# Weight conversion through a PSUM bank, ELU in one VectorE pass, weight sums on GpSimd, and conversions dealt out in three places of a step

## The chip, the cores and the metric

The kernel runs on one core of a Trainium2 chip. The metric is the device time of one execution in microseconds (us). Engines are named as the profile names them: PE is TensorE (matmuls; PEld are its weight loads), DVE is VectorE, ACT is ScalarE, POOL is GpSimd, SP is SyncE, which here only issues DMAs. Each engine works through its own instructions in a fixed order; semaphores make it wait for others.

## What is computed

Attention on 4 x 8 heads (576 positions, 64 wide, with rotary angles), and then two layers on the 2304 resulting rows of 512. Both layers have 2048 hidden units and no bias; all is float32, the inputs of the weights float64:

```python
h = x @ w_in                                            # layer 1
g = np.where(h > 0.0, h, np.exp(np.minimum(h, 0.0)) - 1.0)
x = (g @ w_out).astype(np.float32)
h = x @ w_in2                                           # layer 2
g = h - np.tanh(h)
return (g @ w_out2).astype(np.float32)
```

## The kernel before

The program has three parts, one after the other: attention, layer 1 and layer 2. The matmuls take float32 values as a sum of a high and a low part (a cast, and the difference that the cast leaves), so each product is three matmuls. A split is therefore always a pair: a cast on ACT, and a subtraction on POOL (or DVE).

**Layer 1** works in 96 steps, numbered 0 to 95: four groups of 512 hidden units, in each six blocks of 384 tokens, in each four steps of 128 hidden units. In step i, `emit_f1(i)` makes h for that step in a PSUM bank from pool `ps_h` (twelve matmuls, L447), and `emit_f2(i - 4)` multiplies the finished g of four steps earlier by the second weight into four PSUM banks from pool `ps_y` (twelve matmuls, L481). Every fourth step a token block is complete: `emit_acc` in the next step empties the four y banks into `xa`, on ACT in the first group (L491) and by an addition on DVE later (L493), and the next `emit_f2` needs these banks. Between the two, the ELU of step i runs as exp on ACT into one of two buffers `ft` (`emit_act`, L455), two DVE instructions (`emit_dve`, L460 and L461, emitted a step later), and a split (`split_g`, L464 on ACT and L465 on POOL, two steps later) into one of three buffers `gt`.

**Conversion.** All weights come as float64. A chunk of 512 columns is loaded raw (`load_w`, L64, a DMA on SP into one of two buffers in `fm`), and `conv_part` turns it into float32: part 0 takes the magnitude of the high word on ACT (L74), part 1 clamps and shifts (L76, L77), part 2 puts the sign bits in (L81), part 3 adds the low word's bits (L85), the last three parts on DVE. All read and write `GM`, a region of the SBUF tile `fm`. The result is then split into layer 1's weight memory (`conv_w`, L91 and L92), or split and stored in DRAM for layer 2 (`stage_out`, L91 and L92, then `store`, L509). For layer 2's first weight the sums of quarters of two chunks are stored too (`pair_sums`, L518 to L522, on DVE).

The list `todo` holds this conversion work with a due time in steps; in the loop over the steps everything due by i is emitted at the end of step i, after `emit_dve`, in the order of the due times. What the engines get is that order, and each engine keeps it.

**Layer 2** has 24 steps q: three pairs of token blocks, in each eight pairs of weight chunks. It forms products of sums of blocks (a Strassen-like scheme): seven blocks of six matmuls per q (L701) into four banks, and units of twelve matmuls for the second weight (L669). For each of four results per q, `stage_a` (a square, a mask, a polynomial and tanh on ACT and POOL), `stage_b` (DVE, L726 to L730) and `stage_c` (a split) make h - tanh(h). The mask of small h is an is_lt on POOL (L715). The sums of x blocks and their splits for the next pair of token blocks (`combo_sums`, L571 to L577; `combo_split`, L583 and L584) are in a list `todo2` that is filled in the last two of the eight steps of a pair and emitted by `next_combo`, at most four times a step, and the rest at the end of the last.

## Time and profile before

| | us |
|---|---|
| median of 3 runs (1180.15 to 1181.58) | 1180.58 |
| the profiled execution | 1183.5 |
| its span, first to last instruction | 1181.7 |
| PE busy | 1089.3 (92%) |
| DVE busy | 914.3 (77%) |
| POOL busy | 764.4 (65%) |
| ACT busy | 650.9 (55%) |

The profile is of one execution. Its page gives busy time by engine, the chain of work that ended last, and the costliest groups of instructions. The trace behind it answers further questions: busy times in a chosen stretch, who waited for whom and how long, all instructions of a line with their shortest, median and longest duration, and the instructions in order of time. A line number such as L493 is a line of the kernel before. In the rows, "x4" is a count, and a bracket such as [4.06 <-DVE xa L493] says that the engine sat idle for 4.06 us ahead of that instruction and that the named one ended the wait.

### The profile page before, as it was taken

What the parts mean: (1) busy time and instruction counts of PE and PEld (TensorE: products, weight loads), DVE (VectorE), ACT (ScalarE), POOL (GpSimd) and SP (SyncE); (2) the same over time, 40 slices, a digit from 0 to 9 for tenths busy, and PEclk for the clock granted to TensorE, in tenths of its full rate; (3) what the DMA queues carried; (4) which work ended last, traced back from release to release, by engine and by line L of the source; (5) the groups of instructions that cost most, each with busy time, mean ns of one, the idle gap of its engine ahead of it and who ended that gap; (6) DMA issues with size and microseconds to landing.
All of it is one profiled execution on the core that took longest, in us unless ns stands there. A gap on an engine that the chain in (4) does not pass through costs nothing. (4 is left out here: it accounts for less than half of the span.)

```text
span 1181.7 us, 18751 instructions
## 1 busy us (share of the span) xinstructions
PE 1089.3 (92%) x6512; PEld 970.6 (82%) x6512; DVE 914.3 (77%) x1564; ACT 650.9 (55%) x1418; POOL 764.4 (65%) x662
## 2 busy tenths in 40 slices
PE   2999999999979898989999999979997999799998
PEld 2777777777779897979899999979986998688996
DVE  5888878988477888778889867576787778877784
ACT  2676666776645544333344434366666666657662
POOL 2887887876466745444454545576787777866773
PEclk9999999999998999989999999999998999989999
DMA  7767767675023344243343664253544755536531
GB/s 227 225 180 220 180 179 212 182 223 121 19 90 98 125 142 127 77 138 135 132 133 102 211 212 154 87 189 131 173 158 144 266 176 189 180 99 229 197 118 54
DMA packets 80574, 184.27 MB, mean 156 GB/s; under 512 B 7264, under 2 KB 43104, under 8 KB 80480
## 3 DMA queue, kind: packets, MB, share of 16 engines
q1 hardware_dynamic: 80480, 183.07, 49.4%
q8 instruction: 52, 0.85, 0.3%
q14 instruction: 42, 0.34, 0.1%
HBM read 126.94 MB, written 27.79 MB: 131 GB/s over the span
## 5 line engine op out<-in xcount | busy, mean ns | idle before, releaser
L701 PE MATMUL hb<-blk,wa 128*128 128x384 f32 x1008 | 193.6, 341 | 22.9 <-DVE fm L729 20.0
L701 PEld LDWEIGHTS hb<-blk,wa 128*128 128x128 f32 x1008 | 179.9, 190 | 31.5 <-DVE fm L729 21.9
L252 POOL TENSOR_SCALAR a<-a,r 128x576 f32<-128x576 f32 x144 | 134.5, 945 | 63.9 <-DVE r L249 43.6
L465 POOL TENSOR_TENSOR gt<-ft,gt 128x384 fp32r<-128x384 f32 x96 | 111.6, 1163 | 79.4 <-ACT gt L464 66.9
L669 PE MATMUL y<-wb,blk 128*128 128x512 f32 x603 | 156.6, 397 | 1.0 <-ACT blk L464 0.5
L715 POOL TENSOR_SCALAR fm<-fm 128x384 f32<-128x384 f32 x96 | 124.2, 1294 | 50.1 <-ACT fm L714 41.2
L235 ACT ACTIVATE a<-s,nm 128x576 f32<-128x576 f32 x144 | 106.9, 743 | 88.9 <-DVE nm L221 71.6
L455 ACT ACTIVATE ft<-h 128x384 f32<-128x384 f32 x96 | 47.2, 492 | 178.4 <-POOL gt L465 127.7
L221 DVE TENSOR_REDUCE nm<-s 128x1 f32<-128x576 f32 x144 | 108.2, 753 | 37.5 <-PE s L212 35.9
L669 PEld LDWEIGHTS y<-wb,blk 128*128 128x128 f32 x603 | 114.7, 191 | 24.2 <-POOL blk L465 0.9
L481 PE MATMUL y<-gt,wb 128*128 128x384 f32 x576 | 112.5, 344 | 17.6 <-DVE xa L493 16.0
L481 PE MATMUL y<-gt,wa 128*128 128x384 f32 x576 | 112.9, 345 | 12.5 <-ACT xa L491 6.5
L481 PEld LDWEIGHTS y<-gt,wb 128*128 128x128 f32 x576 | 103.6, 194 | 20.2 <-issue 10.2
L481 PEld LDWEIGHTS y<-gt,wa 128*128 128x128 f32 x576 | 104.4, 195 | 14.8 <-ACT xa L491 7.6
L447 PE MATMUL h<-blk,wa 128*128 128x384 f32 x576 | 109.0, 336 | 4.6 <-ACT blk L54 2.6
L447 PE MATMUL h<-blk,wb 128*128 128x384 f32 x576 | 109.3, 338 | 0.0
L92 POOL TENSOR_TENSOR fm<-fm 128x512 fp32r<-128x512 f32 (+1 forms) x48 | 62.7, 1307 | 69.7 <-ACT fm L91 51.0
L447 PEld LDWEIGHTS h<-blk,wa 128*128 128x128 f32 x576 | 100.9, 189 | 6.3 <-ACT blk L54 2.9
L447 PEld LDWEIGHTS h<-blk,wb 128*128 128x128 f32 x576 | 102.7, 191 | 0.0
L76 DVE TENSOR_SCALAR fm<-fm 128x512 f32<-128x512 f32 x64 | 50.0, 781 | 63.1 <-ACT fm L74 62.7
L465 POOL TENSOR_TENSOR blk<-fm,blk 128x384 fp32r<-128x384 f32 x67 | 73.5, 1097 | 37.0 <-ACT blk L464 35.7
L147 POOL TENSOR_TENSOR t<-t,tabs 128x576 f32<-128x576 f32 x59 | 86.7, 1471 | 8.5 <-DMA t<-in_qk 8.5
(103 smaller groups left out, 2284.2 us busy)
## 6 DMA issues: line engine op xcount, KB each, us to landing
wa<-wi SPq DMA_DIRECT2D x96, 448.0 KB, 5.0
wb<-wo SPq DMA_DIRECT2D x48, 512.0 KB, 6.1
k<-hl SPq DMA_DIRECT2D x64, 288.0 KB, 4.4
t<-in_qk SPq DMA_DIRECT2D x30, 576.0 KB, 6.1
wi<-fm SPq DMA_DIRECT2D x24, 512.0 KB, 4.2
fm<-in_w1i SPq DMA_DIRECT2D x16, 512.0 KB, 3.9
fm<-in_w1o SPq DMA_DIRECT2D x16, 512.0 KB, 4.1
fm<-in_w2i SPq DMA_DIRECT2D x16, 512.0 KB, 3.6
```

The lines of the kernel that those rows point to most:

```text
L76: nc.vector.tensor_scalar(out=f, in0=f, scalar1=LO_CLAMP, scalar2=HI_CLAMP, op0=ALU.max, op1=ALU.min)
L92: nc.gpsimd.tensor_tensor(out=lo, in0=f, in1=hi.bitcast(F32), op=ALU.subtract)
L147: eng.tensor_tensor(out=t[:, i, :], in0=t[:, i, :], in1=tabs[:, i, :], op=ALU.mult)
L221: nc.vector.tensor_reduce(out=nm, in_=s_t[i][:, :, 0:288], axis=AX.XY, op=ALU.max, negate=True)
L235: nc.scalar.activation(out=a.rearrange("p (x c) -> p x c", x=2), in_=s[:, :, 0:288], func=AF.Exp, bias=nm_t.pop(i), scale=1.0, accum_out=den,)
L252: nc.gpsimd.tensor_scalar(out=a, in0=a, scalar1=r[:, x:x + 1], scalar2=1.0, op0=ALU.mult, op1=ALU.mult)
L447: nc.tensor.matmul(out=hp, lhsT=w[:, wp, ws], rhs=x_hl(t, xp, c), start=(m == 0), stop=(m == 3 * KC - 1))
L465: nc.gpsimd.tensor_tensor(out=g[:, 1, :], in0=f, in1=g[:, 0, :].bitcast(F32), op=ALU.subtract)
L481: nc.tensor.matmul(out=y_t[e][:, 0:NB], lhsT=w[:, wp, es], rhs=gt[:, gp, :], start=st, stop=sp)
L669: nc.tensor.matmul(out=y, lhsT=gt[:, gp, es], rhs=w[:, wp, :], start=(k == 0), stop=(k == 11))
L701: nc.tensor.matmul(out=bank, lhsT=w[:, wp, o:o + 128], rhs=x[:, xp, cc, :], start=(start and k == 0), stop=(stop and k == 5), skip_group_c ...
L715: nc.gpsimd.tensor_scalar(out=mask, in0=u, scalar1=U_SMALL, scalar2=None, op0=ALU.is_lt)
```

## The change

- **Conversion.** `conv_ps` replaces `conv_part` outside attention: parts 1 and 2 write a PSUM bank `cvb` instead of `GM`, and part 3 writes `GM` from it. The bank is taken from `ps_h`, which keeps three.
- **ELU.** ACT makes relu(-h) and then exp of its negative, into one of three buffers in `fm` (`ft` is gone); DVE makes max(e - 1, h) in one instruction.
- **Sums of weights.** The four instructions go to POOL, each with its own due time.
- **Stores.** `stage_out` puts only the high part into a staging buffer; the low part overwrites its source in `GM`; a store is two DMAs on SP.
- **Loads.** All but the first two raw loads of layer 1 are issued on ACT's queue.
- **Due times.** They are new, and the list is emptied at three places of a step: after `emit_acc`, after `emit_act`, and at the end.
- **Layer 2.** For two of the four results (C22 and C12) the mask is a relu on ACT. `todo2` is filled in the last five steps of a pair, one item in each of the first four, and seven in the last.

```diff
-    fm = const.tile([128, 5888], F32, name="fm")
+    fm = const.tile([128, 6656], F32, name="fm")
...
-    def load_w(key):
+    def load_w(key, eng=nc.sync):
...
-        nc.sync.dma_start(out=t.bitcast(mybir.dt.int64), in_=w_src[l, kind][c])
+        eng.dma_start(out=t.bitcast(mybir.dt.int64), in_=w_src[l, kind][c])
...
-    ps_h = ctx.enter_context(tc.tile_pool(name="ps_h", bufs=4, space=PSUM))
+    ps_h = ctx.enter_context(tc.tile_pool(name="ps_h", bufs=3, space=PSUM))
+    ps_c = ctx.enter_context(tc.tile_pool(name="ps_c", bufs=1, space=PSUM))
...
     def emit_act(i):
-        f = ft[:, i % 2, :]
-        nc.scalar.activation(out=f, in_=h_t[i], func=AF.Exp)
+        f = fm[:, 5376 + NB * (i % 3):5376 + NB * (i % 3) + NB]
+        nc.scalar.activation(out=f, in_=h_t[i], func=AF.Relu, scale=-1.0)
+        nc.scalar.activation(out=f, in_=f, func=AF.Exp, scale=-1.0)
         f_t[i] = f
 
     def emit_dve(i):
         h, f = h_t.pop(i), f_t[i]
-        nc.vector.tensor_scalar(out=f, in0=f, scalar1=1.0, scalar2=-1.0, op0=ALU.min, op1=ALU.add)
-        nc.vector.scalar_tensor_tensor(out=f, in0=h, scalar=0.0, in1=f, op0=ALU.max, op1=ALU.add)
+        nc.vector.scalar_tensor_tensor(out=f, in0=f, scalar=-1.0, in1=h, op0=ALU.add, op1=ALU.max)
+
+    cvb = ps_c.tile([128, 512], F32, name="cvb")
+
+    def conv_ps(key, part, f):
+        words = raw_t[key].bitcast(U32).rearrange("p (n t) -> p n t", t=2)
+        lo_w, hi_w = words[:, :, 0], words[:, :, 1]
+        cu = cvb.bitcast(U32)
+        if part == 0:
+            nc.scalar.activation(out=f, in_=hi_w.bitcast(F32), func=AF.Abs)
+        elif part == 1:
+            nc.vector.tensor_scalar(out=cvb, in0=f, scalar1=LO_CLAMP, scalar2=HI_CLAMP, op0=ALU.max, op1=ALU.min)
+            nc.vector.tensor_scalar(
+                out=cu, in0=cu, scalar1=3, scalar2=0x3FFFFFFF, op0=ALU.logical_shift_left, op1=ALU.bitwise_and
+            )
+        elif part == 2:
+            nc.vector.scalar_tensor_tensor(
+                out=cu, in0=hi_w, scalar=0xC0000000, in1=cu, op0=ALU.bitwise_and, op1=ALU.bitwise_or
+            )
+        else:
+            nc.vector.scalar_tensor_tensor(
+                out=f.bitcast(U32), in0=lo_w, scalar=29, in1=cu, op0=ALU.logical_shift_right, op1=ALU.bitwise_or
+            )
...
-        split_w(st[:, 0, :].bitcast(F32R), st[:, 1, :].bitcast(F32R), GM[:, cols])
-        staged.append((dst, st))
+        split_w(st.bitcast(F32R), GM[:, cols].bitcast(F32R), GM[:, cols])
+        staged.append((dst, st, GM[:, cols]))
...
-        nc.sync.dma_start(out=dst, in_=st)
+        for k, src in enumerate(parts):
+            nc.sync.dma_start(out=dst[:, k, :], in_=src)
...
-        tt = nc.vector.tensor_tensor
...
+        tt = nc.gpsimd.tensor_tensor
...
+    CP = (0, 0.6, 0.8, 1.0)
...
-            todo += [(t0 + 0.35 * (4 * x + k), conv_part, key, k, GM[:, 512 * x:512 * x + 512]) for k in range(4)]
...
+            todo += [(t0 + 1.4 * x + CP[k], conv_ps, key, k, GM[:, 512 * x:512 * x + 512]) for k in range(4)]
...
+            todo += [(t1 + CP[k], conv_ps, key, k, GM[:, at:at + 512]) for k in range(4)]
...
-            while todo and todo[0][0] <= i:
-                _, f, *arg = todo.pop(0)
-                f(*arg)
+            run(i)
...
-            nc.gpsimd.tensor_scalar(out=mask, in0=u, scalar1=U_SMALL, scalar2=None, op0=ALU.is_lt)
+            if v1:
+                nc.scalar.activation(out=mask, in_=u, func=AF.Relu, scale=-1.0, bias=us)
+            else:
+                nc.gpsimd.tensor_scalar(out=mask, in0=u, scalar1=U_SMALL, scalar2=None, op0=ALU.is_lt)
...
-            if live and pr == NPR - 2 and tp + 1 < NT // 2:
...
+            if live and 3 <= pr and tp + 1 < NT // 2:
```

Before `run(i)`, the loop now also has `run(i - 0.67)` after `emit_acc` and `run(i - 0.33)` after `emit_act`.

The order of the instructions shows what the new due times do. On DVE, around the accumulation of step 40, the kernel before has this (L460 and L461 are the ELU, L76 to L85 a conversion, L493 the accumulation):

```order
L460 TENSOR_SCALAR ft<-ft 128x384
L461 SCALAR_TENSOR_TENSOR ft<-h,ft 128x384
L76 TENSOR_SCALAR fm<-fm 128x512
L77 TENSOR_SCALAR fm<-fm 128x512
L81 SCALAR_TENSOR_TENSOR fm<-fm 128x512
L85 SCALAR_TENSOR_TENSOR fm<-fm 128x512
L493 TENSOR_TENSOR xa<-y,xa 128x384 x4
```

The same place in the changed kernel, whose lines are L462 for the ELU, L473, L474, L478 and L482 for the conversion and L517 for the accumulation:

```order
L462 SCALAR_TENSOR_TENSOR fm<-fm,h 128x384
L478 SCALAR_TENSOR_TENSOR cvb<-fm,cvb 128x512
L482 SCALAR_TENSOR_TENSOR fm<-fm,cvb 128x512
L462 SCALAR_TENSOR_TENSOR fm<-fm,h 128x384
L517 TENSOR_TENSOR xa<-y,xa 128x384 x4
L473 TENSOR_SCALAR cvb<-fm 128x512
L474 TENSOR_SCALAR cvb<-cvb 128x512
```

A whole conversion stood directly ahead of the accumulation; now there is one ELU instruction, behind the end of a conversion, and the next conversion begins after it.

On ACT, in steps 39 and 40, the kernel before has (L464 is the cast of g, L455 the exp, L74 the magnitude, L91 a cast of weights):

```order
L464 CAST gt_4272<-ft 128x384
L455 ACTIVATE ft<-h 128x384
L74 ACTIVATE fm<-fm 128x512
L91 CAST fm<-fm 128x512
L464 CAST gt_4272<-ft 128x384
L455 ACTIVATE ft<-h 128x384
L91 CAST wa<-fm 128x512
```

and the changed kernel, with L456 and L457 for relu and exp, L471 for the magnitude, L488 for the cast of g and L64 for a load:

```order
L64 DMA fm<-in_w1o 128x512
L488 CAST gt_4275<-fm 128x384
L456 ACTIVATE fm<-h 128x384
L457 ACTIVATE fm<-fm 128x384
L91 CAST wa<-fm 128x512
L471 ACTIVATE fm<-fm 128x512
L91 CAST fm<-fm 128x512
L488 CAST gt_4275<-fm 128x384
```

The ELU has two instructions instead of one, the loads have come in from SP's queue, and the casts of weights have moved by one place.

On DVE in layer 2, in the next to last step of a pair of token blocks, the kernel before has these (L571, L573 and L575 are the sums of x; L687 an accumulation; L726 to L730, L817 and L829 work on the results):

```order
L687 TENSOR_TENSOR xa<-y,xa 128x4x128
L571 TENSOR_TENSOR ft<-xa 128x768
L817 TENSOR_TENSOR fm<-hb,fm 128x384
L573 TENSOR_TENSOR xa<-xa 128x2x384
L726 TENSOR_TENSOR fm<-fm 128x384
L729 TENSOR_TENSOR fm<-fm 128x384
L730 COPY_PREDICATED fm<-fm 128x384
L687 TENSOR_TENSOR xa<-y,xa 128x4x128
L575 TENSOR_TENSOR xa<-xa 128x2x384
```

In the changed kernel that step has one sum, L597 (formerly L575), between two results:

```order
L761 COPY_PREDICATED fm<-fm 128x384
L597 TENSOR_TENSOR xa<-xa 128x2x384
L757 TENSOR_TENSOR fm<-hb,fm 128x384
L759 SCALAR_TENSOR_TENSOR fm<-fm 128x384
L760 TENSOR_TENSOR fm<-hb,fm 128x384
L761 COPY_PREDICATED fm<-fm 128x384
L715 TENSOR_TENSOR xa<-y,xa 128x4x128
L849 TENSOR_TENSOR fm<-hb,fm 128x384
```

The other two sums have gone to the two steps ahead of it.

## Rows read from the trace of the kernel before

**Rows 1.** Stretches: busy us (instructions) of PE, PEld, DVE, ACT, POOL; clock, DMA.

```profile
320.80:759.04 438.24, 404.79 (x2246) 398.90 (x2246) 345.20 (x518) 181.24 (x368) 231.04 (x191) 0.97 0.40 131
628.16:661.44 33.28, 33.28 (x193) 33.28 (x193) 30.43 (x48) 13.87 (x27) 18.88 (x15) 1.00 0.46 159
502.40:512.69 10.29, 6.23 (x26) 5.94 (x26) 8.34 (x14) 4.02 (x9) 5.52 (x5) 0.75 0.56 181
```

**Rows 2.** Waits of PE in layer 1: us in total, times, longest.

```profile
PE y L481 <- DVE xa L493: 20.8, 11, 4.1
PE y L481 <- ACT xa L491: 8.1, 4, 2.6
PE h L447 <- ACT blk L54: 2.6, 1, 2.6
PE h L447 <- POOL blk L55: 2.0, 2, 1.4
```

**Rows 3.** In order of time, around step 40: start, duration, engine, line, operation.

```profile
503.07 0.49 ACT L455 ACTIVATE ft<-h 128x384 f32<-128x384 f32 x1 [1.95 <-POOL gt L465]
...
504.14 0.43 DVE L76 TENSOR_SCALAR fm<-fm 128x512 f32<-128x512 f32 x1 [3.23 <-ACT fm L74]
...
505.07 1.63 DVE L81 SCALAR_TENSOR_TENSOR fm<-fm 128x512 uint32<-128x512 uint32 x1
...
508.02 1.94 DVE L493 TENSOR_TENSOR xa<-y,xa 128x384 f32<-128x384 f32 x4
...
508.71 4.18 PE L481 MATMUL y<-gt,wb 128*128 128x384 f32 x12 [4.06 <-DVE xa L493]
```

**Rows 4.** The longest waits of ACT and of DVE in layer 1.

```profile
ACT ft L455 <- POOL gt L465: 127.7, 68, 3.9
...
DVE fm L76 <- ACT fm L74: 62.7, 37, 4.1
```

**Rows 5.** Groups of DVE in layer 1: count, busy us, mean ns, idle before.

```profile
L460 DVE TENSOR_SCALAR ft<-ft 128x384 f32<-128x384 f32 x96 | 56.8, 591 | 16.6 <-ACT ft L455 16.6
...
L81 DVE SCALAR_TENSOR_TENSOR fm<-fm 128x512 uint32<-128x512 uint32 x56 | 49.2, 879 | 1.4
...
L76 DVE TENSOR_SCALAR fm<-fm 128x512 f32<-128x512 f32 x56 | 42.5, 760 | 63.1 <-ACT fm L74 62.7
...
L521 DVE TENSOR_TENSOR fm<-fm 128x256 f32<-128x256 f32 x8 | 7.2, 896 | 0.0
```

**Rows 6.** Single lines in layer 1: shortest/median/longest ns, first and last start.

```profile
L76 DVE TENSOR_SCALAR fm<-fm x56: 416/920/1125, 324.5 to 719.4; 128x512 f32<-128x512 f32 x56
...
L81 DVE SCALAR_TENSOR_TENSOR fm<-fm x56: 681/693/1666, 326.1 to 722.5; 128x512 uint32<-128x512 uint32 x56
...
L465 POOL TENSOR_TENSOR gt<-ft,gt x94: 999/1146/1742, 325.7 to 755.5; 128x384 fp32r<-128x384 f32 x94
...
L92 POOL TENSOR_TENSOR fm<-fm x48: 844/1291/2078, 338.9 to 726.2; 128x512 fp32r<-128x512 f32 x40, 128x256 fp32r<-128x256 f32 x8
```

**Rows 7.** SP's loads of raw weights: waits, and issues (ns, shortest/median/longest).

```profile
L64 SPq EVENT_SEMAPHORE  x80: 17/3804/34552, 295.0 to 707.4; - x80
L64 SPq DMA_DIRECT2D fm<-in_w2o x16: 327/328/339, 406.9 to 709.3; - x16
```

**Rows 8.** Stretches of layer 2, columns as in rows 1.

```profile
759.04:805.62 46.58, 38.84 (x199) 35.82 (x199) 28.58 (x49) 27.72 (x57) 30.39 (x27) 0.96 0.40 141
821.26:852.54 31.28, 31.28 (x157) 28.22 (x157) 23.69 (x39) 20.66 (x43) 23.61 (x21) 1.00 0.54 186
868.18:886.14 17.96, 16.19 (x79) 14.02 (x79) 15.65 (x23) 11.52 (x23) 15.34 (x12) 1.00 0.30 103
886.14:910.68 24.54, 18.09 (x80) 15.93 (x80) 17.85 (x25) 14.07 (x28) 18.99 (x14) 0.86 0.45 153
```

**Rows 9.** In order of time, a change of token pair in layer 2.

```profile
888.71 2.20 DVE L729 TENSOR_TENSOR fm<-fm 128x384 f32<-128x384 f32 x1 [0.91 <-POOL fm L719]
...
898.66 2.29 PE L701 MATMUL hb<-blk,wa 128*128 128x384 f32 x6 [6.45 <-DVE fm L729]
```

More of the change, by code (lines that the diff above doesn't have):

```diff
@@ L428, in attention_elu_tanhshrink @@
     gt3 = fcst.tile([128, 3, 2, NB], F32R, name="gt3")
-    ft = fcst.tile([128, 2, NB], F32, name="ft")
     acc = xa
@@ L515, in pair_sums @@
         s1, s2, s3 = (GM[:, 1024 + 256 * k:1280 + 256 * k] for k in range(3))
[L516 to L522 removed]
+        tt = nc.gpsimd.tensor_tensor
+        out_, a, b, op = (
+            (s1, a21, a22, ALU.add), (s2, s1, a11, ALU.subtract), (s3, a11, a21, ALU.subtract), (a21, a12, s2, ALU.subtract)
+        )[part]
+        tt(out=out_, in0=a, in1=b, op=op)
     def pair_out(pr, part):
@@ L541, in attention_elu_tanhshrink @@
             key = (1, 0, 2 * pr + x)
-            todo += [(t0 + 0.35 * (4 * x + k), conv_part, key, k, GM[:, 512 * x:512 * x + 512]) for k in range(4)]
-        todo += [(t0 + 2.8 + 0.3 * k, pair_sums, k) for k in range(2)]
-        todo += [(t0 + (3.4, 4.6, 5.7, 6.8)[k], pair_out, pr, k) for k in range(4)]
-        for o, at in ((3.5, 0), (5.3, 768), (6.7, 0), (8.0, 1280), (9.3, 768)):
+            todo += [(t0 + 1.4 * x + CP[k], conv_ps, key, k, GM[:, 512 * x:512 * x + 512]) for k in range(4)]
+        todo += [(t0 + 2.75 + 0.4 * k, pair_sums, k) for k in range(4)]
+        todo += [(t0 + (3.96, 4.8, 6.3, 7.65)[k], pair_out, pr, k) for k in range(4)]
+        for o, o2, at in ((4.1, 5.55, 1792), (5.7, 7.0, 0), (7.0, 8.35, 768), (8.2, 9.45, 1280), (9.4, 10.65, 1792)):
             t1 = t0 + o
@@ L550, in attention_elu_tanhshrink @@
                 key = lone_b.pop(0)
-            todo += [(t1 + 0.25 * k, conv_part, key, k, GM[:, at:at + 512]) for k in range(4)]
-            todo.append((t1 + 1.25, conv_w, key, 4, at) if key[0] == 0 else (t1 + 1.25, wo_out, key[2], at))
-    todo += [(x[0] + 0.9, store) for x in todo if x[1] in (pair_out, wo_out)]
+            todo += [(t1 + CP[k], conv_ps, key, k, GM[:, at:at + 512]) for k in range(4)]
+            todo.append((t0 + o2, conv_w, key, 4, at) if key[0] == 0 else (t0 + o2, wo_out, key[2], at))
+    todo += [(x[0] + 0.8, store) for x in todo if x[1] in (pair_out, wo_out)]
     todo.sort(key=lambda x: x[0])
-    order = [x[2] for x in todo if x[1] == conv_part and x[3] == 0]
-    free = [x[0] + 0.2 for x in todo if x[1] == conv_part and x[3] == 3]
-    todo += [(0, load_w, key) for key in order[:2]] + [(t1, load_w, key) for t1, key in zip(free, order[2:])]
+    order = [x[2] for x in todo if x[1] == conv_ps and x[3] == 0]
+    free = [x[0] + 0.3 for x in todo if x[1] == conv_ps and x[3] == 3]
+    todo += [(0, load_w, key, nc.sync) for key in order[:2]] + [(t1, load_w, key, nc.scalar) for t1, key in zip(free, order[2:])]
     todo.sort(key=lambda x: x[0])
@@ L561, in x2 @@
         return xa.rearrange("p (c n) -> p c n", n=NTOK)[:, 2 * k:2 * k + 2, NB * t:NB * t + NB]
-    tms = [fm[:, 0:2 * NB].rearrange("p (a n) -> p a n", a=2), ft, ft]
+    tms = [fm[:, o:o + 2 * NB].rearrange("p (a n) -> p a n", a=2) for o in (0, 5760, 5760)]
     XORD = ("B11", "B21", "T2", "T1", "T3", "T4", "B22")
@@ L619, in attention_elu_tanhshrink @@
         nc.vector.memset(b1, B1)
+        nc.vector.memset(us, U_SMALL)
         nc.vector.memset(g1, G1)
@@ L624, in attention_elu_tanhshrink, with run @@
                (combo_split, 0, "T4", nc.vector), (combo_split, 0, "B22", nc.gpsimd)]
+        def run(until):
+            while todo and todo[0][0] <= until:
+                _, f, *arg = todo.pop(0)
+                f(*arg)
         for i in range(n):
@@ L627, in attention_elu_tanhshrink @@
             emit_acc()
+            run(i - 0.67)
             if i < NJ * (NT - 1):
@@ L632, in attention_elu_tanhshrink @@
             emit_act(i)
+            run(i - 0.33)
             if i >= 1:
                 emit_dve(i - 1)
-            while todo and todo[0][0] <= i:
-                _, f, *arg = todo.pop(0)
-                f(*arg)
+            run(i)
             if i >= n - 11:
@@ L647, in attention_elu_tanhshrink @@
         nq = len(qs)
-        banks = [ps_h.tile([128, 512], F32, tag="h", name="hb")[:, 0:NB] for _ in range(4)]
+        banks = [ps_h.tile([128, 512], F32, tag="h", name="hb")[:, 0:NB] for _ in range(3)] + [cvb[:, 0:NB]]
         tl = {}
```

29 lines of the change are left out of this document (12 added, 17 removed).

## The prediction

> **What bounds the kernel now.** I looked first at TensorE's stretch for layer 1, then at what it waits for there, then at one wait in order of time, and last at layer 2. Layer 1 runs from 320.80 to 759.04 us, 438.24 us [rows 1]. Eight of its steps without a stall take 33.28 us, 4.16 each, with TensorE never idle and the granted clock at 1.00, the 2.4 GHz level [rows 1]. Of the steps in the window, numbers 1 to 3 hold twelve matmuls (half a step, 2.08) and 4 to 95 hold twenty-four, so the same matmuls without a stall would take 3 x 2.08 + 92 x 4.16 = 389.0 us. **49.3 us are lost**, and TensorE is the bound otherwise: a gain can only come from these stalls. The list of its waits names them: 20.8 us for DVE's accumulation L493, 8.1 for ACT's accumulation L491, 2.6 and 2.0 for a block of x [rows 2], together 33.5. The rest is the clock after a stall: step 40 takes 10.29 us instead of 4.16, so 6.13 lost, of which 4.06 is the wait, at a mean granted clock of 0.75, between the 1.2 and the 2.4 GHz level [rows 1, 3]. That is 1.51 us lost per us waited, and 33.5 x 1.51 = 50.6, the 49.3 to within 3%. So all of the loss hangs on these waits.
>
> Why the accumulation is late is seen at step 40 [rows 3]. ACT's exp waits 1.95 us for POOL, which still reads the `ft` buffer that exp wants to write. The magnitude pass L74 stands behind it on ACT, DVE's first conversion instruction L76 sits idle 3.23 us for it, and then four conversion instructions run in one piece (504.14 to 508.02) ahead of L493. TensorE gets the y bank 4.06 us late. The totals have the same shape: ACT's exp waits 127.7 us for POOL over layer 1, DVE's L76 62.7 us for ACT [rows 4].
>
> **What the change takes from each engine in layer 1.** DVE is busy 345.2 us [rows 1]. L460 goes: 56.8 us. The pair sums go to POOL: four groups of eight, the costliest 7.2 us, 21.2 together. The four conversion instructions now take 49.2 (L81), 48.8, 47.0 and 42.5 (L76), together 187.5 [rows 5]. Through PSUM they remain four; no row shows a tensor_scalar into PSUM. Bounds: 0.416, the fastest L76, and 0.92, its median [rows 6]. I take 0.69, since L81 runs the same 512 columns in 0.681 at its fastest, close to its median of 0.693; that makes 56 x 4 x 0.69 = 154.6. DVE comes to 345.2 - 56.8 - 21.2 - 187.5 + 154.6 = 234 us (166 to 286 by the bounds), 60% of 389.
>
> The medians say more than the minima: L76 takes 0.416 at its fastest and 0.92 as a rule, and POOL's split L465 0.999 and 1.146 [rows 6]: both engines hold each other up. The Trainium skill (SBUF — State Buffer, Who interferes with whom) says that a DVE instruction with at most one SBUF input and outside the two-port modes does not contend with GpSimd; the conversions with one PSUM side are of that kind, and what the rows show agrees with the other half of the rule, that in-place SBUF ones do contend. By that rule the 0.69 is firm.
>
> ACT gets a second pass for the ELU, 96 x 0.49 = 47.0 (the exp's duration [rows 3]), and issues 54 loads, 0.328 each by SP's row [rows 7] (bounds 0 and 0.66, twice that), 17.7: 181.2 + 47.0 + 17.7 = 246 us of 389, 63%. POOL gets 32 sums of 256 columns at 0.844, the fastest L92 [rows 6] (0.999 at most, L465's 384 columns): 27 us on 231.0, 66%. No engine is full.
>
> **What lies on the path.** An accumulation costs TensorE nothing if DVE is free for it about 1.5 us into its step: TensorE has 2.08 us of `emit_f1` before the first bank is needed, and one of four accumulations takes about 0.5 (L493 x4 in 1.94 us [rows 3]). After the change at most half a conversion stands ahead of one, as the order around step 40 shows: there a single L462 and a finished conversion. The worst case I find in the order is step 32: h at 2.08, relu 0.49, exp 0.49, magnitude 0.66 (exp's 0.49 scaled from 384 to 512 columns), then two DVE instructions of 0.69: 5.1 us after step 31 began, 0.95 us into step 32, in time. At step 52 a cast stands ahead as well and takes it to about 1.6, 0.1 late. So DVE's 20.8 x 1.51 = 31 us go nearly whole. The waits for ACT and for x, 12.7 x 1.51 = 19 us, lie in the first 28 steps; the third ELU buffer takes away the 127.7 us for which ACT stood before POOL, but ACT also gets the relu and the loads there. I leave a quarter of it, 5 us. **Layer 1: 49.3 - 5 = 44 us gained**, bounds 22 (rival A) and 49.3.
>
> At nothing I cost these. Three h banks instead of four: a bank is asked for again 3 x 4.16 - 2.08 = 10.4 us after its matmuls instead of 14.6, and DVE reads it one step later; the list of waits has no matmul that waits for it [rows 2]; without that cover each us late costs 1.51. Two DMAs for a store, and lo halves that stay in GM until they have landed: SP has lost the loads, and a GM region is asked for over a step later; without the cover ACT waits, as rival A prices. The constant `us` is one memset.
>
> **Layer 2** takes 15.64 us per step when nothing stalls (31.28 for two [rows 8]). At a change of token pair it takes 17.96 and 24.54 us, so 2.3 and 8.9 are lost, twice. The change moves two of the three DVE sums that stand in the step before (L571, L573) one and two steps earlier, and one split on POOL three steps earlier. I take the 2.3 for gone, 4.6 in all, since each of these steps now has one extra instruction instead of three. The 8.9 I leave: its four last splits stay in one step, where DVE's L729 takes 2.20 us and TensorE then waits 6.45 us for an L729 [rows 9]; what stands there on DVE and POOL is not touched. Half of the masks move from POOL to ACT, some 0.5 us twice per step (exp's 0.49 [rows 3]). Two undisturbed steps have ACT busy 20.66 of 31.28 us [rows 8]; with four masks 22.7. I cost this at nothing but the last step, 0.5 us; if the chain ACT to DVE had no slack it would be 24 x 0.5 = 12. The start of layer 2 (46.58 us [rows 8]) I leave as it is. **Layer 2: 4.6 - 0.5 = 4 us**, bounds -8 and +13 (half of the 8.9 twice on top).
>
> **Sum.** 44 + 4 = 48 us. The profiled execution took 1183.5 us, so it would take 1135.5; it is 2.9 over the median of 1180.58, and from the median the forecast is 1132.5.
>
> **Rivals.** *A: ACT's queue takes DVE's place.* The loads now stand on ACT, each waiting for DVE's last conversion instruction, and relu and exp behind it; the magnitude pass waits for the load's landing there too. For it: on SP the same loads waited a median of 3.8 us [rows 7]. Against it: they stand a third of a step after the instruction they wait for. If half of layer 1's 44 us stay, 1180.6 - 22 - 4 = 1154.5.
>
> *B: the conversions gain nothing from PSUM.* The Trainium skill (VectorE: DVE Perf Modes, Why PSUM operands drop a tier) says that fp32 with a PSUM operand falls to the single rate; the fastest L76 at 0.416 against L81's 0.681 [rows 6] agrees that there is a double rate to lose. As a mechanism of this kernel: the two tensor_scalars rise by 0.27 each over what they take now, so DVE is at 345.2 - 56.8 - 21.2 + 56 x 0.54 = 297 us, 76%, and first halves of 2 us instead of 1.4 pass the 1.5 us at some accumulations. A third of DVE's 31 us would stay: 1142.5.
>
> *C: the crossings ease too*, since POOL has fewer masks there and DVE comes to them less late. With half of 8.9 gone twice: 1123.5.
>
> *D: slower than before.* If every load holds ACT as long as it held SP, 54 x 3.8 = 205 us, ACT needs 246 + 205 = 451 us for layer 1, more than the 438.2 of now: 1180.6 + 13 - 4 = 1189.5. It decides from (438.2 - 246) / 54 = 3.6 us per load on. Against it: most of SP's wait is its having reached the load early, which the later place takes away.
>
> *E: nothing happens*, because the stalls at the accumulations have a cause that I do not see: 1180.
>
> **How the numbers follow.** Forecast 0.60 (its own range 1124 to 1145), A 0.17, B 0.08, C 0.06, D 0.05, E 0.04. The range 1120 to 1156 takes in the forecast, B, nearly all of C and the nearer half of A, about 0.8. A measurement of this kernel tells 0.2%, some 2.4 us, from no change: faster 0.91, same 0.04, slower 0.05.
>
> **What would show it.** Right: steps of 4.16 us nearly throughout layer 1 and a stretch of about 394 us; no wait of a y matmul for DVE over 1 us; conversion instructions at 0.69 with median and minimum together; no wait of ACT for POOL ahead of the ELU; two stalls at the crossings instead of four. Wrong: L64 or L471 on ACT waiting microseconds with relu behind them (A, D); tensor_scalars over 0.9 in PSUM (B); h matmuls waiting for DVE (the three banks); layer 2's undisturbed steps over 15.64.

## The result and the profile after

The changed kernel takes **1133.24 us** (median of 4 runs, 1132.62 to 1133.92); the kernel before takes 1181.08 beside it. The ratio is 0.9594, 95% interval 0.9577 to 0.961: 4% faster. The profiled run took 1133.38 us with a span of 1131.6. The forecast was 1132.5, in a range of 1120 to 1156.

These are the stretches of the changed kernel that answer to [rows 1] and [rows 8], with the same columns: layer 1, step 40, the step before the first change of token pair, the step of the change, and an undisturbed step of layer 2.

```profile
321.82:712.54 390.72, 389.77 (x2245) 388.91 (x2245) 237.06 (x390) 230.01 (x464) 233.13 (x222) 1.00 0.46 147
479.18:483.34 4.16, 4.16 (x25) 4.16 (x25) 3.90 (x7) 2.77 (x6) 3.34 (x3) 1.00 0.36 137
821.54:837.40 15.86, 15.86 (x79) 14.05 (x79) 14.51 (x22) 12.02 (x25) 11.97 (x9) 1.00 0.35 116
837.40:861.09 23.69, 17.39 (x80) 15.34 (x80) 17.77 (x23) 15.41 (x30) 14.48 (x11) 0.86 0.45 159
1043.24:1058.88 15.64, 15.64 (x79) 14.11 (x79) 11.38 (x19) 12.11 (x26) 9.54 (x9) 1.00 0.69 251
```

Layer 1 is 390.72 us long, down from 438.24: 1.8 us above the 389.0 of matmuls without a stall, where 49.3 were lost. Step 40 is back from 10.29 us to 4.16. The clock of the stretch is 1.00, the 2.4 GHz level, instead of 0.97. Layer 2, from 712.54 us to the end, takes 419.04 us instead of 422.67. With a start of layer 1 that came 1.0 us later, the gain in span is 47.5 + 3.6 - 1.0 = 50.1 us, from 1181.7 to 1131.6. The medians differ by 47.8 us; the profiled execution of the kernel before was 2.9 us above its median.

The waits of TensorE in layer 1 (us in total, times, longest), all that is left of [rows 2]:

```profile
PE h L448 <- POOL blk L55: 0.6, 1, 0.6
PE h L448 <- ACT blk L54: 0.2, 1, 0.2
```

Both stand in one place, step 4; the eleven waits for VectorE's accumulation and the four for ScalarE's are gone. The other two engines of [rows 4], ScalarE and VectorE in the same stretch:

```profile
ACT fm L456 <- PE h L448: 110.4, 77, 1.8
ACT gt L488 <- PE y L505: 13.0, 24, 0.8
ACT fm L456 <- POOL gt L489: 7.5, 4, 3.4
ACT fm L456 <- POOL fm L543: 7.2, 4, 1.8
...
DVE cvb L473 <- ACT fm L471: 95.9, 48, 4.7
DVE fm L462 <- ACT fm L457: 30.4, 18, 3.6
DVE xa L517 <- PE y L505: 11.4, 7, 3.0
```

ScalarE stood 127.7 us waiting for GpSimd's split of g ahead of the ELU, now 7.5; another 7.2 us are new, behind the sums of weights that GpSimd has got (L543). The prediction had announced that none would be left; no accumulation is late for these. ScalarE now stands 110.4 us for the h matmuls, and VectorE stands 11.4 us for the y matmuls ahead of its accumulation: they wait for TensorE and not it for them. VectorE's waits for the magnitude pass grew from 62.7 to 95.9 us and cost nothing: none of TensorE's waits stands behind them.

In order of time around step 40, which begins at 479.18 us, as in [rows 3]:

```profile
474.32 0.55 DVE L462 SCALAR_TENSOR_TENSOR fm<-fm,h 128x384 f32<-128x384 f32 x1
...
477.82 2.12 DVE L517 TENSOR_TENSOR xa<-y,xa 128x384 f32<-128x384 f32 x4 [2.95 <-PE y L505]
...
479.18 2.24 PE L448 MATMUL h<-blk,wb 128*128 128x384 f32 x12
...
479.86 0.68 DVE L473 TENSOR_SCALAR cvb<-fm 128x512 f32<-128x512 f32 x1
...
480.57 0.70 DVE L474 TENSOR_SCALAR cvb<-cvb 128x512 uint32<-128x512 uint32 x1
...
481.26 2.24 PE L505 MATMUL y<-gt,wb 128*128 128x384 f32 x12
481.31 0.69 DVE L478 SCALAR_TENSOR_TENSOR cvb<-fm,cvb 128x512 uint32<-128x512 uint32 x1
```

No conversion stands ahead of the accumulation any more. VectorE is done with an ELU instruction, sits idle 2.95 us for the first y bank, and begins to accumulate at 477.82, 1.36 us before step 40 begins; in the kernel before it began 5.62 us into the step. The next conversion follows it, and the y matmuls start at 481.26, right behind the h matmuls.

### The profile page after: what moved, and what is told of

Same layout as the page of the kernel before. It is cut to its first block, busy times and chain, and to the rows that moved or that the text cites. A ratio compares the mean times of both kernels' runs of the same rounds, so it can differ in the third digit from the quotient of the medians.

```text
span 1131.6 us, 18884 instructions
## 1 busy us (share of the span) xinstructions
PE 1075.9 (95%) x6512; PEld 962.2 (85%) x6512; DVE 801.9 (71%) x1437; ACT 724.2 (64%) x1562; POOL 704.9 (62%) x646
## 4 chain that ended last, share of the span: by engine, by line
PE 74%; DVE 15%; ACT 5%; issue 2%; DMA 1%; POOL 1%; SPq 1%; DVEq 0%; ACTq 0%; POOLq 0%
PE y L505 18%; PE h L448 17%; PE y L697 11%; PE o L326 8%; PE hb L729 7%; PE s L212 6%; PE pt L292 4%; PE cvb L729 3%; DVE nm L221 2%; DVE fm L760 2%; DVE fm L757 2%; DVE fm L761 2%; DVE fm L759 1%; DVE xa L715 1%; DMA k<-hl 1%
## 5 line engine op out<-in xcount | busy, mean ns | idle before, releaser
L489 POOL TENSOR_TENSOR gt<-fm,gt 128x384 fp32r<-128x384 f32 x119 | 124.1, 1043 | 60.9 <-ACT gt L488 58.1
L729 PE MATMUL hb<-blk,wa 128*128 128x384 f32 x720 | 142.3, 342 | 7.3 <-DVE fm L760 6.9
L729 PEld LDWEIGHTS hb<-blk,wa 128*128 128x128 f32 x720 | 129.3, 191 | 12.9 <-DVE fm L760 8.6
L456 ACT ACTIVATE fm<-h 128x384 f32<-128x384 f32 x96 | 47.3, 493 | 126.1 <-PE h L448 110.4
L505 PE MATMUL y<-gt,wb 128*128 128x384 f32 x576 | 107.6, 334 | 1.3 <-DVE xa L517 1.3
L473 DVE TENSOR_SCALAR cvb<-fm 128x512 f32<-128x512 f32 x56 | 38.9, 695 | 98.4 <-ACT fm L471 95.9
L505 PE MATMUL y<-gt,wa 128*128 128x384 f32 x576 | 107.7, 334 | 0.1
L750 POOL TENSOR_TENSOR fm<-fm 128x384 f32<-128x384 f32 x48 | 54.5, 1135 | 69.5 <-ACT fm L749 69.5
L489 POOL TENSOR_TENSOR blk<-fm,blk 128x384 fp32r<-128x384 f32 x67 | 70.9, 1059 | 40.8 <-ACT blk L488 39.5
L92 POOL TENSOR_TENSOR fm<-fm 128x512 fp32r<-128x512 f32 (+1 forms) x48 | 58.2, 1219 | 56.3 <-ACT fm L91 55.1
L326 PE MATMUL o<-aT,v 128*64 128x256 f32 (+1 forms) x768 | 89.5, 340 | 2.6 <-ACT aT L268 2.4
```

What stands on the lines that cost most here:

```text
L92: nc.gpsimd.tensor_tensor(out=lo, in0=f, in1=hi.bitcast(F32), op=ALU.subtract)
L326: nc.tensor.matmul(out=o[sl, 0:n], lhsT=w, rhs=m, start=(c == 0), stop=(c == 4))
L489: nc.gpsimd.tensor_tensor(out=g[:, 1, :], in0=f, in1=g[:, 0, :].bitcast(F32), op=ALU.subtract)
L505: nc.tensor.matmul(out=y_t[e][:, 0:NB], lhsT=w[:, wp, es], rhs=gt[:, gp, :], start=st, stop=sp)
L729: nc.tensor.matmul(out=bank, lhsT=w[:, wp, o:o + 128], rhs=x[:, xp, cc, :], start=(start and k == 0), stop=(stop and k == 5), skip_group_c ...
L750: nc.gpsimd.tensor_tensor(out=w, in0=w, in1=u, op=ALU.mult)
```

## The experiments

"Lost" is the length of layer 1 less 388.96 us, the exact form of the prediction's 389.0; the length runs from the first h matmul of step 1 to the first block of layer 2. Before loses 49.3 us, the changed kernel 1.8. Each loss is from one profile, but it repeats: the changed kernel and the three runs below that alter only layer 2 lose 1.7 to 1.8. Times are medians; ratios are to the kernel before on the same chip. That kernel's median was 1185.6 us beside "One place", "Conversion in SBUF", "The old ELU" and "Two ELU buffers", and 1181.7 beside the others, so the parts are priced by what is lost and not by comparing ratios. Line numbers of experiments can be off by one to three from the changed kernel's.

### Undoing one part of the change

**One place instead of three.** The due conversions are issued only at the end of a step.

```
-            run(i - 0.67)
...
-            run(i - 0.33)
```

> The changed kernel (1133.2 us), but the list of conversion work is emptied only at the end of a step; due times, PSUM bank, ELU and buffers as changed. The prediction's theory, that a stall needs more than about 1.5 us of late DVE work directly ahead of an accumulation: at six accumulations a first half and the sign pass now wait for a magnitude pass of the same step, each about 0.3 us late, so 3 us more, 1136 (1134 to 1140), layer 1 393 to 397 us. Rival, that the three places are what removed the stalls: 15 us or more of the 47.5 come back, 1148 and up.

Measured: 1136.05 us, ratio 0.9589 (0.9561 to 0.9617); lost 5.1 us, in small pieces of 0.2 to 1.7 in eight steps, as the expectation had it; the rival is out. The two extra places are worth 3.3 us beside all the rest. The order as a whole (due times and places) was not undone.

**Conversion in SBUF.** Still the changed kernel's due times, but the converted halves stay in SBUF.

```
-        cu = cvb.bitcast(U32)
+        cu = f.bitcast(U32)
...
-            nc.vector.tensor_scalar(out=cvb, in0=f, ...)
+            nc.vector.tensor_scalar(out=f, in0=f, ...)
```

> The changed kernel, but the conversion works in place in SBUF as before (the PSUM bank is allocated and unused). The prediction's theory, that the four instructions fall from 3.34 to 2.78 us per conversion because they no longer share with POOL: the two tensor_scalars show a median of 0.9 and a minimum of 0.42 again, DVE is busy some 30 us more, POOL's split L489 goes from 1.04 to 1.1 or more; few accumulations are hit, 4 us more, 1137 (1134 to 1143). Rival, that the contention was the cause of the stalls: 20 us or more come back, 1153 and up. Second rival, the rule that an SBUF operand pair runs at the double rate and PSUM at the single one: less DVE time than with PSUM, 1133 or below.

Measured: 1139.41 us, ratio 0.9615 (0.9581 to 0.9649); lost 7.5. The conversion's groups on VectorE in layer 1 (count, busy us, mean ns, idle before), first of this run, then of the changed kernel:

```profile
L478 DVE SCALAR_TENSOR_TENSOR fm<-fm 128x512 uint32<-128x512 uint32 x56 | 69.0, 1233 | 1.4
L474 DVE TENSOR_SCALAR fm<-fm 128x512 uint32<-128x512 uint32 x56 | 55.8, 997 | 1.9
L482 DVE SCALAR_TENSOR_TENSOR fm<-fm 128x512 uint32<-128x512 uint32 x56 | 53.0, 946 | 1.4
```

```profile
L474 DVE TENSOR_SCALAR cvb<-cvb 128x512 uint32<-128x512 uint32 x56 | 39.2, 699 | 1.9
...
L478 DVE SCALAR_TENSOR_TENSOR cvb<-fm,cvb 128x512 uint32<-128x512 uint32 x56 | 38.8, 693 | 1.4
L482 DVE SCALAR_TENSOR_TENSOR fm<-fm,cvb 128x512 uint32<-128x512 uint32 x56 | 38.4, 685 | 2.0
```

With L473 (39.6 us in SBUF, 38.9 through PSUM) the conversion takes 217 us in SBUF and 155 through the bank. So the bank takes 62 us from VectorE, where some 30 were expected, and 5.7 us of that show as time. The second rival, that the conversion is shorter in SBUF, is out. TensorE's longest wait here is not for VectorE's accumulation (0.5 us in all) but for GpSimd's split of x:

```profile
PE h L448 <- POOL blk L55: 2.7, 3, 1.1
```

**The old ELU.** One exponential on ScalarE and two instructions on VectorE, three buffers kept.

```
-        nc.scalar.activation(out=f, in_=h_t[i], func=AF.Relu, scale=-1.0)
-        nc.scalar.activation(out=f, in_=f, func=AF.Exp, scale=-1.0)
+        nc.scalar.activation(out=f, in_=h_t[i], func=AF.Exp)
...
-        nc.vector.scalar_tensor_tensor(out=f, in0=f, scalar=-1.0, in1=h, ...)
+        nc.vector.tensor_scalar(out=f, in0=f, scalar1=1.0, scalar2=-1.0, ...)
+        nc.vector.scalar_tensor_tensor(out=f, in0=h, scalar=0.0, in1=f, ...)
```

> The changed kernel, but the ELU is exp on ACT and two instructions on DVE as before, with three buffers. The prediction's theory, that DVE's 57 us matter only where they stand ahead of an accumulation: 0.36 to 0.6 us more ahead of each, 3 us more, 1136 (1133 to 1141); ACT 47 us less busy. Rival, that DVE's load is what made the stalls: DVE at 290 of 390 us, a third of the stalls back, 1149.

Measured: 1133.16 us, ratio 0.9566 (0.9537 to 0.9595); lost 1.3, where 3 us more than in the changed kernel were expected. Layer 1 of this run:

```profile
320.35:710.57 390.22, 389.51 (x2245) 388.93 (x2245) 290.10 (x486) 184.63 (x368) 236.45 (x223) 1.00 0.46 147
```

VectorE is busy 290.10 us here and 237.06 in the changed kernel. Beside the PSUM bank the ELU with one VectorE pass is worth nothing, although it takes 53 us from VectorE.

**Both at once.** Conversion in SBUF and the old ELU, the two diffs above together.

> The changed kernel with both of VectorE's reliefs undone at once: the conversion goes on in SBUF in place, and the ELU is one exponential and two VectorE instructions, as before; all else stays. Undone singly they cost 5.7 us and -0.5 us of layer 1 (lost above its floor: 7.5 and 1.3 us, where the changed kernel loses 1.8). Theory that each does what it does alone: layer 1 loses 7.0 us and the run takes 1138.5 us. Theory that either is spare for the other, since VectorE is the engine that runs short only when both are gone (its busy time in layer 1 then is back at about 365 us of 390, where the changed kernel has 250): layer 1 loses 15 to 22 us, the run takes 1147 to 1154 us, and TensorE waits for VectorE's halves of x at L517 and for its reads of the h banks.

Measured: 1155.14 us, ratio 0.9761 (0.9727 to 0.9795); lost 24.6. Singly they cost 5.7 and -0.5 us, together 22.8. The rival is right, a little above its range, and the theory that the parts add up falls. Layer 1 of this run, and TensorE's waits in it:

```profile
320.33:733.89 413.56, 397.20 (x2246) 391.46 (x2245) 355.85 (x486) 182.28 (x368) 258.76 (x223) 0.99 0.43 138
```

```profile
PE y L505 <- DVE xa L517: 9.0, 8, 1.9
PE h L448 <- POOL blk L55: 4.5, 4, 1.8
PE h L448 <- DVE fm L462: 1.6, 2, 1.1
```

VectorE is busy 356 us here, 91% of the 389 of matmuls (the changed kernel's 237 us stand beside that, not the 250 of the expectation), and the waits for its accumulation are back. With one of the two reliefs it has some 60 us less to do (290 and 297 us), and that is enough. Not all of the loss goes through VectorE: 4.5 us are waits for GpSimd's split of x, which is slower too with the conversion in SBUF (1.12 us on average, 1.02 in the changed kernel).

**Two ELU buffers.** All else as changed.

```
-        f = fm[:, 5376 + NB * (i % 3):5376 + NB * (i % 3) + NB]
+        f = fm[:, 5376 + NB * (i % 2):5376 + NB * (i % 2) + NB]
```

> The changed kernel, but the ELU has two buffers again instead of three, so relu of step i waits for POOL's split of step i - 2. The prediction's theory, that this wait held ACT back and with it DVE: ACT's relu waits for POOL tens of us in total again; with DVE unloaded only part of it reaches the accumulations, 6 us more, 1139 (1135 to 1147). Rival, that the buffers never mattered and the wait was time ACT had to spare: 1133, within 1 us.

Measured: 1154.74 us, ratio 0.9748 (0.972 to 0.9776); lost 22.2, of which 17.4 in steps 8, 12 and 20. ScalarE's and TensorE's waits in layer 1:

```profile
ACT fm L456 <- POOL gt L489: 134.3, 73, 3.8
```

```profile
PE y L505 <- ACT xa L515: 8.4, 4, 2.9
PE h L448 <- POOL blk L55: 3.1, 3, 1.4
PE y L505 <- DVE xa L517: 1.9, 2, 1.2
```

ScalarE's stand before GpSimd is back (127.7 us before), and with it the waits for ScalarE's accumulation (8.1 before), though VectorE has all its relief. The expectation of 1139 was far too low: the buffer alone is worth 20.4 us.

**Loads on SyncE's queue again.**

```
-    todo += ... [(t1, load_w, key, nc.scalar) for t1, key in zip(free, order[2:])]
+    todo += ... [(t1, load_w, key, nc.sync) for t1, key in zip(free, order[2:])]
```

> The changed kernel with the raw weight loads issued by SyncE's queue again, as before; all else stays. Theory: who issues the loads decides nothing, since the loads are due early and ScalarE has 140 us idle in layer 1: 1133 us, within 2, layer 1 losing 1.8 within 2. Rival: the loads on ScalarE's queue kept later output and input transfers on SyncE's from holding them up (before, the loads of the last weights landed behind such transfers), so that with SyncE they come late again: layer 1 loses 5 to 8 us and the run takes 1136 to 1140 us.

Measured: 1131.49 us (1131.0 to 1132.96), ratio 0.9562 (0.9529 to 0.9595); lost 0.4. Neither helped nor needed, as the theory had it. The 1.4 us less of loss stand in one step. On ScalarE in the changed kernel, in order of time:

```profile
326.93 0.53 ACT L457 ACTIVATE fm<-fm 128x384 f32<-128x384 f32 x1
328.97 0.40 ACTq L64 DMA_DIRECT2D fm<-in_w1i  x1
329.41 0.51 ACT L54 CAST blk<-xa 128x384 fp32r<-128x384 f32 x1 [1.95 <-DVE fm L462]
```

ScalarE's first load stands until 328.97 for the conversion that still reads its buffer (L482, which ends at 328.94): of the 1.95 us of idle time 1.5 are this wait and 0.40 the issue. The cast of an x block stands behind it, and TensorE waits for that block: the 0.2 and 0.6 us above. With the load on SyncE the same cast runs right away and both waits are gone. It is rival A in one place. The difference of the medians, 1.75 us, is under the 2.4 that can be told from none.

**Combination work as before.** The sums and splits of the next token pair stand again in the last two steps of a pair of token blocks.

```
-            if live and 3 <= pr and tp + 1 < NT // 2:
+            if live and pr == NPR - 2 and tp + 1 < NT // 2:
...
```

> The changed kernel with the combination work of layer 2 (sums and splits of the next token pair's blocks) spread as before, over the last two steps of a token pair and not over five; all else stays. Theory: the 2.3 us that the step before each crossing lost comes back, twice, less the 0.2 to 0.5 us that the three early steps lose now: 2.8 to 4.6 us, 1136 to 1138 us. Rival: the gain of layer 2 lay in the mask or elsewhere: 1133 us.

Measured: 1136.08 us, ratio 0.9597 (0.9558 to 0.9636). Layer 2 takes 422.34 us instead of 419.04. The step before the first change of token pair, to be held against 15.86 above:

```profile
820.62:838.21 17.59, 15.90 (x79) 14.05 (x79) 15.65 (x23) 12.63 (x26) 12.13 (x9) 1.00 0.31 105
```

It loses 1.95 us again (before: 2.3), so the spread is what took that stall away. In the steps ahead of the two changes it is worth 2.1 us. The other 1.2 of the 3.3 us stand in the steps of the changes themselves, and their sum varies by 0.9 us among the runs with the changed layer 2 and by 2.1 among those with the old one.

**All masks on GpSimd.**

```
-            if v1:
-                nc.scalar.activation(out=mask, in_=u, func=AF.Relu, scale=-1.0, bias=us)
-            else:
-                nc.gpsimd.tensor_scalar(out=mask, in0=u, scalar1=U_SMALL, ...)
+            nc.gpsimd.tensor_scalar(out=mask, in0=u, scalar1=U_SMALL, ...)
```

> The changed kernel with the mask of small u in layer 2's first part on GpSimd for every pair of units, as before; ScalarE no longer makes half of them. Theory: undisturbed steps stay at 15.64 us and the crossings at 8 to 9 us over that, so the run takes 1133 us, within 1; the last step's tail, where the ScalarE mask stands in the chain, is shorter by about 0.5 us. Rival: GpSimd's relief is what eased the steps around a crossing, so without it their excess grows by 1.5 to 2.5 us each: 1136 to 1138 us.

Measured: 1129.9 us (1128.9 to 1130.92), ratio 0.9547 (0.9513 to 0.958). Both theories miss: it is 3.3 us faster than the changed kernel, and in the profiled runs 2.5 of it lie in layer 2 (416.54 us against 419.04; 1.4 lie ahead of layer 1, which starts 320.0 to 321.8 us into the span from run to run, whatever the kernel). The last step but one of the first token pair, in the changed kernel and then here:

```profile
805.37:821.54 16.17, 15.93 (x79) 14.08 (x79) 13.01 (x21) 11.38 (x24) 8.62 (x8) 1.00 0.68 245
```

```profile
804.66:820.30 15.64, 15.64 (x80) 14.11 (x79) 12.99 (x21) 10.22 (x22) 11.14 (x11) 1.00 0.72 253
```

and the instruction of VectorE that waits for ScalarE at its start, in the same order:

```profile
806.08 1.06 DVE L757 TENSOR_TENSOR fm<-fm 128x384 f32<-128x384 f32 x1 [2.81 <-ACT fm L751]
```

```profile
804.80 1.08 DVE L754 TENSOR_TENSOR fm<-fm 128x384 f32<-128x384 f32 x1 [2.31 <-ACT fm L748]
```

The mask (0.62 us each) stands in ScalarE's chain ahead of what VectorE needs: VectorE starts 0.71 us into the step and not 0.14, and its work then runs without a gap to the L760 that TensorE waits for. In an undisturbed step (15.64 us) this is covered. In the three steps ahead of each change of token pair TensorE loses 0.2 to 0.5 us each, 1.85 in all. With the masks on GpSimd none of the three loses anything. With the combination work as before the first two of them lose nothing either, so that loss takes both parts of the change. The tail is 0.7 us shorter. These two make up the 2.5 us; the start and the steps of the changes differ by 0.9 us each, one way and the other. So this part of the change costs time.

### Building up from the kernel before

**A third ELU buffer alone.** To make room, low halves stay in `GM` until the store, and the old due times let the next conversion overwrite some of them before they are stored. So this kernel leaves wrong low halves in layer 2's weights and serves for its time alone.

```
-        f = ft[:, i % 2, :]
+        f = ft[:, i % 3, :] if i % 3 < 2 else fm[:, 5504:5888]
```

> The kernel before, with a third ELU buffer (and, to make room for it, the changed staging of stores: low halves stay in GM). Two buffers cost the changed kernel 21.5 us, nearly all in steps 8 to 20. If the third buffer frees ACT and nothing else is needed for the first group, layer 1's loss falls from 49.3 us by the 19 to 20 of steps 4 to 28, and part of DVE's 29 goes too, since the magnitude passes come earlier: lost 20 to 28 us, 1154 to 1162. Rival, that the buffers tell only where DVE is already unloaded: lost 44 or more, 1176 and up.

Measured: 1191.15 us, ratio 1.0068 (1.0045 to 1.0091); lost 56.2. Slower by 0.7%, where a gain of some 20 us was expected. ScalarE's 127.7 us before GpSimd are gone here too (6.4 left), but others came instead. A wait of VectorE and one of ScalarE in layer 1:

```profile
DVE fm L76 <- DMA wi<-fm: 28.9, 6, 6.8
```

```profile
ACT wb L91 <- DVE fm L85: 38.8, 13, 4.6
```

The first has no counterpart in the kernel before and comes from the low halves in place: a conversion stands until a store has read its buffer. The second (13.7 us before) is ScalarE, early now, in front of conversions that the old order keeps in one piece. TensorE's waits for VectorE's accumulation stay, 21.2 us (20.8 before). How much of the 6.9 us more is the store's and how much the order's, this run doesn't tell, so it is no measure of the buffer. A version with a staging place of its own was not run. The next two go around this.

**Only the order.** Due times, three places and staging of the changed kernel; conversion in SBUF, old ELU with two buffers, sums on VectorE, loads on SyncE, layer 2 as before. The diff against the changed kernel is the undoing of its other parts, as shown above, and `tt = nc.vector.tensor_tensor` in the sums. The three h banks stay, and the PSUM bank is there unused.

> The kernel before in conversion (in SBUF), ELU (two DVE instructions, two buffers), sums (DVE), loads (SP) and all of layer 2; changed only in the due times, the three places of a step and the staging of stores. If the order clears the accumulations and the buffers the first group, steps 32 to 88 lose 8 us instead of 29 and steps 4 to 28 keep their 20: lost 28, 1160 (1152 to 1168). Rival, that without the lighter DVE the order clears nothing: lost 40 or more, 1172 and up.

Measured: 1169.23 us, ratio 0.989 (0.9858 to 0.9923); lost 33.8. TensorE's waits in layer 1:

```profile
PE y L505 <- DVE xa L517: 9.0, 7, 3.0
PE y L505 <- ACT xa L515: 7.0, 3, 2.4
```

Of the 20.8 us of waits for VectorE's accumulation 9.0 are left; those for ScalarE's (8.1) are nearly untouched. The loss lies between the expectation (28) and its rival (40 or more), and 1169 is just outside the range: steps 32 to 88 still lose 14 us, where 8 were expected.

**Order and third buffer.** The same with `i % 3`.

> As b_order with the third ELU buffer: conversion in SBUF, ELU in two DVE instructions, sums on DVE, loads on SP, layer 2 as before. If buffer and order are the two causes and PSUM, one-pass ELU and sums on POOL are reserves, layer 1 loses 8 to 12 us and the time is 1141 (1137 to 1146). Rival, that DVE's relief (345 to 250 us busy) is the cause: lost 30 or more, 1160 and up.

Measured: 1156.35 us, ratio 0.9777 (0.9749 to 0.9804); lost 22.6. The waits of TensorE now:

```profile
PE y L505 <- DVE xa L517: 9.6, 5, 2.5
PE h L448 <- DVE fm L462: 3.2, 3, 1.9
```

The wait for ScalarE's accumulation is gone from the list and VectorE's stays, so the buffer is for ScalarE and x, as the prediction had it, and VectorE's last 13 us need its relief. The expected 1141 held the relief for worth less than it is, and the rival's 30 us or more are not reached. The three banks of h (3.2 us) are waited for where VectorE reads them late, here and in the run with both reliefs undone.

In layer 1 this run differs from that one only in the sums of weights and the loads, which are as before here and as changed there; they lose 22.6 and 24.6 us. So with VectorE's two reliefs gone, moving the sums to GpSimd gains nothing that shows. In the changed kernel this part was not undone alone.

The staircase in layer 1, then: 49.3 lost, 33.8 with the order, 22.6 with the buffer, 1.8 with VectorE's relief (PSUM bank, ELU, sums) and the loads moved: steps of 15.5, 11.2 and 20.8 us. A step's height depends on what is there already: the buffer is worth 11.2 us here and 20.4 where VectorE has its relief.

### A further step

**Three splits later.** The changed kernel, with the last three splits of the combination left for the step after the change of token pair, where they are needed.

```
-                while todo2 and pr == NPR - 1:
+                while len(todo2) > 3 and pr == NPR - 1:
```

> The changed kernel, but the last three of the seven splits at a change of token pair (T3 and T4 on DVE, B22 on POOL) are emitted in the next step, one at each of its first three places. The stall of 6.3 us at steps 8 and 16 of layer 2 ends with an L760 on DVE that stands behind T3 and T4 (2.7 us) and behind L760 and L761 of 2.2 and 2.1 us that wait for POOL's splits. If that chain is the cause, those two steps lose 3 to 4 us each instead of 8.05 and 9.19: 1123 (1119 to 1128). Rival, that the wait only moves to the matmuls that read T3, T4 and B22: 1133, within 2 us.

Measured: **1124.54 us** (1124.0 to 1126.2), ratio 0.9511 (0.9484 to 0.9537), faster than both kernels: 1124.54 / 1133.24 = 0.992 of the changed one. The two steps lose 4.3 and 4.9 us instead of 8.05 and 9.19, a little more than the 3 to 4 expected, and the rival is out. The step of the change, against 23.69 above:

```profile
835.71:855.69 19.98, 17.53 (x80) 15.41 (x79) 15.08 (x22) 14.87 (x30) 13.48 (x10) 0.91 0.52 188
```

What it avoids is this stretch of the changed kernel, in order of time, the crossing that [rows 9] show of before:

```profile
841.81 1.91 POOL L606 TENSOR_TENSOR blk<-xa,blk 128x768 fp32r<-128x768 f32 x1 [0.20 <-ACT blk L605]
842.06 2.11 DVE L761 COPY_PREDICATED fm<-fm 128x384 f32<-128x384 uint32 x1
...
845.13 0.94 DVE L606 TENSOR_TENSOR blk<-fm,blk 128x768 fp32r<-128x768 f32 x1
845.99 1.75 DVE L606 TENSOR_TENSOR blk<-xa,blk 128x768 fp32r<-128x768 f32 x1
...
849.17 0.56 DVE L760 TENSOR_TENSOR fm<-cvb,fm 128x384 f32<-128x384 f32 x1
849.78 2.29 PE L729 MATMUL cvb<-blk,wa 128*128 128x384 f32 x6 [6.30 <-DVE fm L760]
```

VectorE has two splits (0.94 and 1.75 us) ahead of the L760 that TensorE waits 6.30 us for, and a predicated copy of 0.6 us elsewhere in this layer takes 2.11 beside GpSimd's split. Together with all masks on GpSimd it may gain more; that was not run.

## Why the prediction was right

**What bounds it.** That all 49.3 us of layer 1 hang on the named waits holds: with the waits gone, so are 47.5 of them. The price of 1.51 us lost per us waited holds roughly: the runs that lose 5 us or more pay 1.4 to 1.8. The 0.8 us left in step 4 cost 1.36, or 1.7 each, and there the granted clock stays at 1.00, so it is not the clock alone that makes a wait dearer than its length.

**VectorE's sum.** 234 us were worked out, 237.06 measured. (By its own terms the lower bound is 173 and not 166.) The conversion is 155.3 us against 154.6, its instructions 0.69 on average, with median and minimum together as announced, here L478 of the changed kernel and of the run with the conversion in SBUF (shortest/median/longest ns, first and last start):

```profile
L478 DVE SCALAR_TENSOR_TENSOR cvb<-fm,cvb x56: 685/695/697, 327.5 to 674.6; 128x512 uint32<-128x512 uint32 x56
```

```profile
L478 DVE SCALAR_TENSOR_TENSOR fm<-fm x56: 675/1386/1767, 326.6 to 678.2; 128x512 uint32<-128x512 uint32 x56
```

The same work takes 0.68 us at best either way; in SBUF this line is mostly held up, through PSUM never. The Trainium skill (SBUF — State Buffer, Who interferes with whom) has it that a VectorE instruction with at most one SBUF input, outside the two-port modes, does not contend with GpSimd, and one with two SBUF inputs does; the trace agrees with both halves. The Trainium skill's rule in rival B (VectorE: DVE Perf Modes, Why PSUM operands drop a tier), that fp32 with a PSUM operand has only the single rate, agrees with the trace too: L473 takes at least 0.410 us in SBUF and at least 0.682 through the bank. What failed in B is the conclusion: the bank costs the tensor_scalars their best case and gives all four instructions a sure duration.

**The other engines.** ScalarE's busy time is 230.0 us, and 54 loads of 0.33, which the profile doesn't count as busy, add 18: 248 against 246. GpSimd was put at 258 and is 233.13, since the sums take 0.735 and not 0.844 each, and its splits got faster as well (L489 takes 1.035 us on average, 1.166 before as L465, 1.198 with the conversion in SBUF): the relief works both ways, and only one way was in the sum.

**The path in layer 1.** The gain was put at 44 us and is 47.5. The mis-sized term is the residue, 5 us for ScalarE and x against 1.8. Of these, 1.36 are the first load on ScalarE's queue (gone with the loads on SyncE, lost 0.4) and 0.40 are step 52, the very step that the order had shown 0.1 late. The split of the loss, 31 us for VectorE and 19 for ScalarE and x, stands up to the runs: without the third buffer 20.4 come back, without VectorE's relief 22.8. That the order takes care of the rest of VectorE's share is argued, not shown: alone it took 15.5 us off the kernel before, and it was never undone whole. Rivals A and D are out: of the loads on ScalarE's queue one reaches TensorE, with 0.8 us. E is out with the waits, and C too: the steps of the changes still lose 8.05 and 9.19 us. What the prediction had not seen is that VectorE was relieved twice: either the bank or the ELU would have done, to within 6 us.

**Nothing for the three banks.** Right in the changed kernel (no matmul waits for L462), and its condition, VectorE in time, shows in the runs without relief (waits of 3.2 and 1.6 us).

**Layer 2.** 4 us were forecast, 3.6 measured, but by other terms, so that they agree is luck. The 2 x 2.3 us of the steps before the changes became 2 x 0.93, spread over three steps; the steps of the changes lose 8.05 and 9.19 instead of 8.9 and 9.0, the start is 0.8 shorter, and the tail 0.65 longer (forecast 0.5). So 2.8 + 0.7 + 0.8 - 0.65 = 3.6. Only the first and the last of these terms repeat. Six of the runs above leave layer 2 as in the changed kernel, and the start (its first three steps) takes 45.7 to 47.3 us in the seven profiles, the first step of a change loses 7.9 to 8.4; before and in the three runs with the old layer 2 they are 46.6 to 47.0 us and 8.05 to 9.4. The whole of layer 2 takes 419.0 to 421.1 us in the seven, 420.2 on average, and 421.7 to 423.7 in the four, 422.9 on average: a gain of 2.6 us rather than 3.6. The term that was mis-sized is the mask: costed at 0.5 us, worth 2.5, because the cover of an undisturbed step was taken for all steps, also those that got an extra sum by this same change. With the masks on GpSimd the steps before the changes lose nothing, which is the 4.6 us that was forecast for the spread.

**The sum from the median.** 48 us were subtracted from 1180.58; the medians differ by 47.8, the spans by 50.1. The losses were read from a profile 2.9 us above the median, and the gain of layer 1 was put 3.5 us too low: that these two nearly cancel, and the forecast comes within 1 us, is luck. The mechanism of layer 1 is not.
